# Local attention beside a gated MLP: sixteen half-position units with interleaved logits, and the first fold over the taps on GpSimd

## The chip, the cores and the metric

The kernel runs on one core of a Trainium2 chip. The metric is the device time of one execution in microseconds. The engines are TensorE (PE in the profile, its weight loads PEld), VectorE (DVE), ScalarE (ACT), GpSimd (POOL) and SyncE (SP), whose queue issues most of the transfers. Each engine works through its own instructions in the order in which they stand in the program, and waits at an instruction until the semaphores that it needs have come.

## The reference

```python
def _A_ref(x, wqkv, wo):                       # S 2048, D 512, 32 heads of 16
    q, k, v = ...                              # x @ wqkv, split by head
    idx = pos[:, None] - (jnp.arange(8) * 2)[None, :]      # eight taps, two positions apart
    logits = jnp.einsum("bhsd,bhswd->bhsw", q, k[idx]) * scale   # masked where idx < 0
    o = jnp.einsum("bhsw,bhswd->bhsd", _softmax(logits), v[idx])
    return o.reshape(B, S, D) @ wo

def _B_ref(x, w_in, w_sp, b_sp, w_out):        # F 1792, half of it 896
    z = _gelu(x @ w_in)
    z1, z2 = z[..., :Fh], _layernorm(z[..., Fh:])
    g = jnp.einsum("ts,bsf->btf", w_sp, z2) + b_sp[None, :, None]
    return (z1 * g) @ w_out

xn = _layernorm(x)
out = x + _A_ref(xn, wqkv, wo) * silu(_B_ref(xn, w_in, w_sp, b_sp, w_out))
```

Every position attends to itself and to seven positions before it, each two further back. There is no long product in this attention: its sums are short, and they are made with elementwise operations, one head of 16 channels at a time.

## The kernel before

All matrix products are made from a high and a low part of each float32 operand, three matmuls in place of one (high by high, high by low, low by high). ScalarE rounds the high part (`split`, L183) and VectorE subtracts to get the low part (L184). Weights pass through four raw buffers and eight pairs of split buffers (`weight_pair`, `fetch`, `prep`). The stages are, in the order of TensorE's work: the QKV products (L371 to L373), written to memory in `qkv_d`; z1 (L578 to L580); z2 with its layer norm (L606 to L627), whose statistics end with four small operations on GpSimd (L620 to L623); the spatial product in blocks (`three`, L695), partly by sums of blocks; the projection by `w_out` (`proj`, named b, L910 to L912); and the projection of attention by `wo` (also `proj`, named s), by groups of four position slots in the order 0, 2, 3, 1, each loaded with `load_o` (L678) from `o_d`.

Positions lie as `(p j)`: partition p holds positions 16 p to 16 p + 15, and j from 0 to 15 is the slot. The attention works on eight sets of 64 channels (four heads each), one after the other, in `attention(sub)`. It loads q, and windows of k and v with 14 positions of halo. For each of four groups of four slots it multiplies all eight taps of k by q (L503, tile `pr`, 128x2048) and sums each head's 16 channels (L506). Then it makes the softmax over the taps for all sixteen slots at once (L513 to L525, the exponential on ScalarE at L521). Then, for each group of four slots, it multiplies the taps of v by the weights (L530, in the same buffer `pr`), folds eight taps to four (L536), to two (L537) and to one (L538), transposes in blocks of 32 (L545), and stores with four transfers to `o_d` (L548).

The order of instructions on each engine is worked out when the kernel is built, from priorities. The attention has the lowest one (`LOW`), so it fills VectorE where nothing for TensorE is due. All of the attention's tiles have one buffer, `tt` has two.

Of the kernel before, what the change touches and what calls it, by code (L numbers as in the profile page):

```python
# [11 lines left out]
F32 = mybir.dt.float32  # L12
F32R = mybir.dt.float32r
AF = mybir.ActivationFunctionType
ALU = mybir.AluOpType
AX = mybir.AxisListType

P = 128
# [3 lines left out]
H, DH, W, DIL = 32, 16, 8, 2  # L22
NT = S // P
# [10 lines left out]
NSUB = 8  # L34
CS = D // NSUB
Q = 32
HS = CS // DH
NBLK = GC // CS
HALO = (W - 1) * DIL
NJ = 4  # L40
PAD = 16
WIN = NT + HALO
EPS = 1e-5
MASKED = -1e9 * float(DH) ** 0.5
LOW = 1_000_000
# [4 lines left out]
SYNC = mybir.DependencyInfo(mybir.DependencyClass.Sync, mybir.DependencyReason.DATA)  # L50
# [4 lines left out]
def kernel(  # L55
# [13 lines left out]
    nc = tc.nc  # L69
# [20 lines left out]
    qkv_d = dram.tile([3 * NSUB, S + PAD, CS], F32, name="qkv_d")  # L90
# [6 lines left out]
    o_d = dram.tile([NSUB, NT // NJ, CS, P // Q, NJ * Q], F32, name="o_d")  # L97
# [11 lines left out]
    mask = const.tile([P, W, NT], F32, name="mask")  # L109
# [363 lines left out]
        return t.rearrange("p (i t) -> p i t", i=2)[:, :n]  # L473

    ap_ = ctx.enter_context(tc.tile_pool(name="att", bufs=1))
    at_priority = [LOW]

    def attention(sub):
        saved = tc.cur_priority
        tc.cur_priority = at_priority[0]  # L480
        q = ap_.tile([P, NT, CS], F32, tag="q", name=f"q_{sub}")
        kw = ap_.tile([P, WIN, CS], F32, tag="k", name=f"k_{sub}")
        vw = ap_.tile([P, WIN, CS], F32, tag="v", name=f"v_{sub}")

        def window(t):
            b = qkv_d[3 * sub + t, PAD - HALO :, :]
            return bass.AP(tensor=b.tensor, offset=b.offset, ap=[[NT * CS, P], [1, WIN * CS]])

        nc.sync.dma_start(kw.rearrange("p r c -> p (r c)"), window(1))
        nc.sync.dma_start(q, qkv_d[3 * sub, PAD:, :].rearrange("(p j) c -> p j c", j=NT))  # L490
        nc.sync.dma_start(vw.rearrange("p r c -> p (r c)"), window(2))

        def taps(t, j0):
            b = t[:, j0 : j0 + 1, :]
            return bass.AP(
                tensor=b.tensor, offset=b.offset, ap=[list(b.ap[0]), [DIL * CS, W], [1, NJ * CS]]
            )

        lg = ap_.tile([P, W, NT * HS], F32, tag="lg", name=f"lg_{sub}")
        for j0 in range(0, NT, NJ):  # L500
            pr = ap_.tile([P, W, NJ * CS], F32, tag="pr", name=f"pr_{sub}_{j0}")
            qb = q[:, j0 : j0 + NJ, :].rearrange("p j c -> p (j c)")
            nc.vector.tensor_tensor(  # L503
                pr, taps(kw, j0), qb.unsqueeze(1).to_broadcast([P, W, NJ * CS]), op=ALU.mult
            )
            nc.vector.tensor_reduce(  # L506
                lg[:, :, j0 * HS : (j0 + NJ) * HS],
                pr.rearrange("p w (i d) -> p w i d", d=DH),
                axis=AX.X,
                op=ALU.add,  # L510
            )
        lgv = lg.rearrange("p w (j h) -> p w j h", h=HS)
        nc.vector.tensor_tensor(  # L513
            lgv, lgv, mask.unsqueeze(3).to_broadcast([P, W, NT, HS]), op=ALU.add
        )
        mx = ap_.tile([P, NT * HS], F32, tag="mx", name=f"mx_{sub}")
        nc.vector.tensor_reduce(mx, lg.rearrange("p w i -> p i w"), axis=AX.X, op=ALU.max)
        nc.vector.tensor_tensor(
            lg, lg, mx.unsqueeze(1).to_broadcast([P, W, NT * HS]), op=ALU.subtract
        )  # L520
        nc.scalar.activation(lg, lg, AF.Exp, scale=float(DH) ** -0.5)  # L521
        sm = ap_.tile([P, NT * HS], F32, tag="sm", name=f"sm_{sub}")
        nc.vector.tensor_reduce(sm, lg.rearrange("p w i -> p i w"), axis=AX.X, op=ALU.add)
        nc.vector.reciprocal(sm, sm)
        nc.vector.tensor_tensor(  # L525
            lg, lg, sm.unsqueeze(1).to_broadcast([P, W, NT * HS]), op=ALU.mult
        )
        for j0 in range(0, NT, NJ):
            pr = ap_.tile([P, W, NJ * CS], F32, tag="pr", name=f"pv_{sub}_{j0}")
            nc.vector.tensor_tensor(  # L530
                pr.rearrange("p w (i d) -> p w i d", d=DH),
                taps(vw, j0).rearrange("p w (i d) -> p w i d", d=DH),
                lg[:, :, j0 * HS : (j0 + NJ) * HS].unsqueeze(3).to_broadcast([P, W, NJ * HS, DH]),
                op=ALU.mult,
            )
            nc.vector.tensor_tensor(pr[:, 0:4], pr[:, 0:4], pr[:, 4:8], op=ALU.add)  # L536
            nc.vector.tensor_tensor(pr[:, 0:2], pr[:, 0:2], pr[:, 2:4], op=ALU.add)  # L537
            nc.vector.tensor_tensor(  # L538
                pr[:, 2].rearrange("p (b j c) -> p j b c", b=CS // Q, j=NJ),
                pr[:, 0].rearrange("p (j b c) -> p j b c", b=CS // Q, j=NJ),  # L540
                pr[:, 1].rearrange("p (j b c) -> p j b c", b=CS // Q, j=NJ),
                op=ALU.add,
            )
            tt = ap_.tile([P, CS // Q, NJ * Q], F32, tag="tt", name=f"tt_{sub}_{j0}", bufs=2)
            nc.vector.transpose(tt.rearrange("p b x -> p (b x)"), pr[:, 2])  # L545
            for a in range(P // Q):
                dst = o_d[sub, j0 // NJ, :, a]
                nc.sync.dma_start(  # L548
                    dst.rearrange("(b c) x -> c b x", c=Q), tt[a * Q : (a + 1) * Q]
                )  # L550
        at_priority[0] = tc.cur_priority
        tc.cur_priority = saved

    for sub in range(NSUB):
        attention(sub)

    def block_sums(i):
        top, low = t4(f"sa_{i}"), t4(f"sb_{i}")
# [52 lines left out]
    def spatial_block(c, js):  # L611
        return prep(w_sp[c, js], CT, f"wsp_{c}_{js}")
# [104 lines left out]
    for c in (2, 3):  # L717
        for n, js in enumerate(order):
            w = spatial.get((c, js)) or spatial_block(c, js)
# [11 lines left out]
        for f0 in range(0, FB, 2):  # L731
            n = min(2, FB - f0)
# [183 lines left out]
    for i, j in enumerate(rows_of):  # L916
        c, jj = divmod(j, JC)
# [29 lines left out]
    for i in range(0, NT, 2):  # L947
        j0 = rows_of[i]
# [67 lines left out]
```

## Time and profile before

| | before |
|---|---|
| median of two timed runs | 708.0 us (707.93 and 708.08) |
| span of the profiled execution | 706.6 us |
| TensorE busy | 700.7 us, 3152 matmuls |
| VectorE busy | 619.2 us |
| ScalarE busy | 260.9 us |
| GpSimd busy | 41.8 us |
| moved by transfers | 151.93 MB |

The span reaches from the first to the last instruction of one profiled execution; no separate time of that execution is given, so it stands beside the median of the timed runs, 1.4 us below it. A group's row in the profile gives line, engine, operation, tiles and shapes, the count, then the busy time in us and the mean in ns, then the engine's idle time just before these instructions and what ended it. A row of the timeline gives the start in us, the duration in us, engine, line and operation. A row of waits gives who waited for whom, the total in us, how often, and the longest. Engine and share rows are told where they stand.

### The profile page before, as it was taken

What the parts mean: (1) busy time and instruction counts of PE and PEld (TensorE: products, weight loads), DVE (VectorE), ACT (ScalarE), POOL (GpSimd) and SP (SyncE); (2) the same over time, 40 slices, a digit from 0 to 9 for tenths busy, and PEclk for the clock granted to TensorE, in tenths of its full rate; (3) what the DMA queues carried; (4) which work ended last, traced back from release to release, by engine and by line L of the source; (5) the groups of instructions that cost most, each with busy time, mean ns of one, the idle gap of its engine ahead of it and who ended that gap; (6) DMA issues with size and microseconds to landing.
All of it is one profiled execution on the core that took longest, in us unless ns stands there. A gap on an engine that the chain in (4) does not pass through costs nothing.

```text
span 706.6 us, 8920 instructions
## 1 busy us (share of the span) xinstructions
PE 700.7 (99%) x3152; PEld 585.4 (83%) x3152; DVE 619.2 (88%) x770; ACT 260.9 (37%) x403; POOL 41.8 (6%) x81
## 2 busy tenths in 40 slices
PE   8999999999999999999999999999999999999997
PEld 7888888888888988888888888888888888888886
DVE  6774599989998899989999999999999999799665
ACT  4343332343224466751112211354545542131531
POOL 3100000000000443320000000000000000000000
PEclk9999999999999999999999999999999999999999
DMA  8767775585785131579956742877857781353996
GB/s 271 255 189 228 240 242 178 161 287 207 258 275 220 33 135 69 190 255 323 328 183 219 288 135 60 307 239 260 276 200 269 246 260 59 125 165 101 303 327 235
DMA packets 96652, 151.93 MB, mean 215 GB/s; under 512 B 8672, under 2 KB 50912, under 8 KB 96608
## 3 DMA queue, kind: packets, MB, share of 16 engines
q1 hardware_dynamic: 57968, 108.77, 47.1%
q10 hardware_dynamic: 38640, 42.60, 17.3%
q8 instruction: 24, 0.39, 0.2%
q14 instruction: 20, 0.16, 0.1%
HBM read 100.40 MB, written 50.94 MB: 214 GB/s over the span
## 4 chain that ended last, share of the span: by engine, by line
PE 98%; DMA 1%; DVE 0%; SPq 0%; issue 0%
PE g L695 22%; PE q L695 12%; PE p L695 6%; PE qkv L371 6%; PE qkv L373 6%; PE qkv L372 6%; PE z L608 4%; PE z L607 4%; PE z L606 4%; PE z L580 4%; PE b L911 4%; PE z L578 4%; PE b L910 4%; PE b L912 4%; PE z L579 4%; PE s L911 2%
## 5 line engine op out<-in xcount | busy, mean ns | idle before, releaser
L503 DVE TENSOR_TENSOR pr<-k,q 128x2048 f32<-128x2048 f32 x32 | 73.2, 2286 | 1.9 <-DMA q<-qkv_d 1.5
L530 DVE TENSOR_TENSOR pv<-v,lg 128x2048 f32<-128x2048 f32 x32 | 73.3, 2291 | 0.9
L506 DVE TENSOR_REDUCE lg<-pr 128x128 f32<-128x2048 f32 x32 | 73.0, 2281 | 0.4
L391 ACT ACTIVATE stage<-qkv 128x512 f32<-128x512 f32 x36 | 21.4, 596 | 49.2 <-PE qkv L373 49.1
L536 DVE TENSOR_TENSOR pv<-pv 128x1024 f32<-128x1024 f32 x32 | 39.1, 1221 | 0.5
L608 PE MATMUL z<-w_0h,BIG 128*128 128x512 f32 x64 | 25.0, 391 | 0.0
L607 PE MATMUL z<-w_0l,BIG 128*128 128x512 f32 x64 | 25.0, 391 | 0.0
L606 PE MATMUL z<-w_0h,BIG 128*128 128x512 f32 x64 | 24.9, 389 | 0.0
L921 ACT ACTIVATE bt<-b 128x512 f32<-128x512 f32 x16 | 9.4, 597 | 41.5 <-PE b L912 41.5
L627 ACT ACTIVATE zt<-zt,nmz,mvz 128x896 f32<-128x896 f32 x16 | 17.9, 1134 | 17.6 <-POOL nmz L623 17.3
L267 DVE TENSOR_TENSOR xT<-xT,mr 128x512 f32<-128x512 f32 x20 | 13.8, 688 | 11.2 <-DMA mr<-mv_d 6.6
L537 DVE TENSOR_TENSOR pv<-pv 128x512 f32<-128x512 f32 x32 | 22.0, 687 | 0.6
L608 PE MATMUL z<-w_1h,BIG 128*128 128x384 f32 x64 | 21.5, 336 | 0.0
L606 PE MATMUL z<-w_1h,BIG 128*128 128x384 f32 x64 | 21.5, 335 | 0.0
L607 PE MATMUL z<-w_1l,BIG 128*128 128x384 f32 x64 | 21.4, 335 | 0.0
L587 ACT ACTIVATE z1t<-z 128x512 f32<-128x512 f32 x21 | 12.5, 594 | 21.8 <-PE z L580 21.8
L965 DVE TENSOR_TENSOR sg<-s,sg 128x512 f32<-128x512 f32 (+1 forms) x17 | 11.2, 657 | 10.6 <-PE s L912 9.7
L618 DVE BATCH_NORM_STATS2 zst<-zt 128x6 f32<-128x448 f32 x32 | 19.1, 610 | 1.5 <-ACT zt L609 1.5
L620 POOL TENSOR_TENSOR nmz<-mvz,mone 128x1 f32<-128x1 f32 x16 | 5.0, 315 | 234.8 <-DVE mvz L619 234.7
L184 DVE TENSOR_TENSOR BIG<-zt,BIG 128x896 fp32r<-128x896 f32 x16 | 17.1, 1079 | 1.1 <-ACT BIG L183 1.1
L609 ACT ACTIVATE zt<-z 128x512 f32<-128x512 f32 (+1 forms) x24 | 12.8, 535 | 13.4 <-PE z L608 12.1
L373 PE MATMUL qkv<-wqkv_0h,BIG 128*128 128x512 f32 x43 | 16.7, 389 | 0.0
(543 smaller groups left out, 2164.1 us busy)
## 6 DMA issues: line engine op xcount, KB each, us to landing
qkv_d<-stage ACTq DMA_DIRECT2D x24, 512.0 KB
k<-qkv_d SPq DMA_DIRECT2D x8, 960.0 KB
v<-qkv_d SPq DMA_DIRECT2D x8, 960.0 KB
z_d<-z1t ACTq DMA_DIRECT2D x14, 512.0 KB
t_d<-zt ACTq DMA_DIRECT2D x16, 384.0 KB
zl<-z_d SPq DMA_DIRECT2D x12, 512.0 KB
tr<-t_d SPq DMA_DIRECT2D x16, 384.0 KB
x<-in_x SPq DMA_DIRECT2D x16, 256.0 KB
```

What stands on the lines that cost most here:

```text
L371: nc.tensor.matmul(pq, xh[:, k], wh, start=k == 0, stop=False)
L372: nc.tensor.matmul(pq, xh[:, k], wl, start=False, stop=False)
L373: nc.tensor.matmul(pq, xl[:, k], wh, start=False, stop=k == KB - 1)
L503: nc.vector.tensor_tensor(pr, taps(kw, j0), qb.unsqueeze(1).to_broadcast([P, W, NJ * CS]), op=ALU.mult)
L506: nc.vector.tensor_reduce(lg[:, :, j0 * HS : (j0 + NJ) * HS], pr.rearrange("p w (i d) -> p w i d", d=DH), axis=AX.X, op=ALU.add,)
L530: nc.vector.tensor_tensor(pr.rearrange("p w (i d) -> p w i d", d=DH), taps(vw, j0).rearrange("p w (i d) -> p w i d", d=DH), lg[:, :, j0 * ...
L536: nc.vector.tensor_tensor(pr[:, 0:4], pr[:, 0:4], pr[:, 4:8], op=ALU.add)
L606: nc.tensor.matmul(pz, xh[:, k], wh, start=k == 0, stop=False)
L607: nc.tensor.matmul(pz, xh[:, k], wl, start=False, stop=False)
L608: nc.tensor.matmul(pz, xl[:, k], wh, start=False, stop=k == KB - 1)
L695: nc.tensor.matmul(pg, z[a], w[b], start=start and i == 0, stop=stop and i == 2, skip_group_check=seeded)
L911: nc.tensor.matmul(pp[:, cols], hi, wl, start=False, stop=False)
```

## The change

The eight sets of channels become sixteen units: each set is cut into its slots 0 to 7 and 8 to 15. A unit loads half of q and windows of k and v with 22 instead of 30 positions per partition, and makes its softmax over eight slots. The units overlap: while unit u makes its weighted sums, the logits of unit u + 1 are made between them, one group of four slots at a time. For that, `pv` (weighted products) gets a buffer of its own beside `pr` (products of logits), `lg` gets two buffers, and `tt` goes from two buffers to one. The first fold, eight taps to four, moves from VectorE to GpSimd, and a dependency is added by hand so that it starts after the following unit's product of logits, beside the sum over channels. The rest of a weighted sum (`finish`) follows after that sum over channels.

```diff
+        def first_fold(part, after=None):
+            pv = part[2]
+            ins = nc.gpsimd.tensor_tensor(pv[:, 0:4], pv[:, 0:4], pv[:, 4:8], op=ALU.add)
+            if after is not None:
+                tc.add_manual_dep(ins.ins, after.ins.name, SYNC, reason="beside the sum over channels")
...
-            nc.vector.tensor_tensor(pr[:, 0:4], pr[:, 0:4], pr[:, 4:8], op=ALU.add)
...
-            tt = ap_.tile([P, CS // Q, NJ * Q], F32, tag="tt", name=f"tt_{sub}_{j0}", bufs=2)
+            tt = ap_.tile([P, CS // Q, NJ * Q], F32, tag="tt", name=f"tt_{u}_{j0}", bufs=TTB)   # TTB = 1
...
+        def start(u):
+            load_qk(u)
+            lgs[u] = ap_.tile([P, W, NH * HS], F32, tag="lg", name=f"lg_{u}", bufs=2)
+
+        start(0)
+        for j0 in range(0, NH, NJ):
+            heads(0, j0, scores(0, j0)[0])
+        load_v(0)
+        softmax(0)
+        part = None
+        for u in range(len(units)):
+            more = u + 1 < len(units)
+            if more:
+                start(u + 1)
+            for j0 in range(0, NH, NJ):
+                if more:
+                    pr, ins = scores(u + 1, j0)
+                    if part:
+                        first_fold(part, ins)
+                    heads(u + 1, j0, pr)
+                elif part:
+                    first_fold(part)
+                if part:
+                    finish(part)
+                part = weighted(u, j0)
+            if more:
+                load_v(u + 1)
+                softmax(u + 1)
+        first_fold(part)
+        finish(part)
```

`scores` is the product of L503 and `heads` the sum of L506, `weighted` the product of L530, and `finish` holds L537 to L548; in `softmax` the operations of L513 to L525 stand as they were, on half the slots.

More of the change, by code (lines that the diff above doesn't have):

```diff
@@ L41 @@
 PAD = 16
-WIN = NT + HALO
+NH = NT // 2
+HWIN = NH + HALO
+TTB = 1
 EPS = 1e-5
@@ L475, with attention, window, load_qk @@
     ap_ = ctx.enter_context(tc.tile_pool(name="att", bufs=1))
-    at_priority = [LOW]
-    def attention(sub):
+    def attention():
         saved = tc.cur_priority
[L480 to L491, printed above, removed]
+        tc.cur_priority = LOW
+        units = [(sub, h) for sub in range(NSUB) for h in range(2)]
+        qs, ks, vs, lgs = {}, {}, {}, {}
+        def window(sub, t, h):
+            b = qkv_d[3 * sub + t, PAD - HALO + h * NH :, :]
+            return bass.AP(tensor=b.tensor, offset=b.offset, ap=[[NT * CS, P], [1, HWIN * CS]])
+        def load_qk(u):
+            sub, h = units[u]
+            ks[u] = ap_.tile([P, HWIN, CS], F32, tag="k", name=f"k_{sub}_{h}")
+            qs[u] = ap_.tile([P, NH, CS], F32, tag="q", name=f"q_{sub}_{h}")
+            nc.sync.dma_start(ks[u].rearrange("p r c -> p (r c)"), window(sub, 1, h))
+            nc.sync.dma_start(
+                qs[u],
+                qkv_d[3 * sub, PAD:, :].rearrange("(p j) c -> p j c", j=NT)[:, h * NH : (h + 1) * NH],
+            )
+        def load_v(u):
+            sub, h = units[u]
+            vs[u] = ap_.tile([P, HWIN, CS], F32, tag="v", name=f"v_{sub}_{h}")
+            nc.sync.dma_start(vs[u].rearrange("p r c -> p (r c)"), window(sub, 2, h))
         def taps(t, j0):
@@ L497, in taps, with scores, heads @@
             )
[L499 to L504, printed above, removed]
-            )
+        def scores(u, j0):
+            pr = ap_.tile([P, W, NJ * CS], F32, tag="pr", name=f"pr_{u}_{j0}")
+            qb = qs[u][:, j0 : j0 + NJ, :].rearrange("p j c -> p (j c)")
+            ins = nc.vector.tensor_tensor(
+                pr, taps(ks[u], j0), qb.unsqueeze(1).to_broadcast([P, W, NJ * CS]), op=ALU.mult
+            )
+            return pr, ins
+        def heads(u, j0, pr):
             nc.vector.tensor_reduce(
-                lg[:, :, j0 * HS : (j0 + NJ) * HS],
+                lgs[u][:, :, j0 * HS : (j0 + NJ) * HS],
                 pr.rearrange("p w (i d) -> p w i d", d=DH),
@@ L511, in attention @@
             )
[L512 to L533, printed above, removed]
+        def softmax(u):
+            sub, h = units[u]
+            n = NH * HS
+            lg = lgs[u]
+            lgv = lg.rearrange("p w (j h) -> p w j h", h=HS)
+            mk = mask[:, :, h * NH : (h + 1) * NH]
+            nc.vector.tensor_tensor(
+                lgv, lgv, mk.unsqueeze(3).to_broadcast([P, W, NH, HS]), op=ALU.add
+            )
+            mx = ap_.tile([P, n], F32, tag="mx", name=f"mx_{u}")
+            nc.vector.tensor_reduce(mx, lg.rearrange("p w i -> p i w"), axis=AX.X, op=ALU.max)
+            nc.vector.tensor_tensor(
+                lg, lg, mx.unsqueeze(1).to_broadcast([P, W, n]), op=ALU.subtract
+            )
+            nc.scalar.activation(lg, lg, AF.Exp, scale=float(DH) ** -0.5)
+            sm = ap_.tile([P, n], F32, tag="sm", name=f"sm_{u}")
+            nc.vector.tensor_reduce(sm, lg.rearrange("p w i -> p i w"), axis=AX.X, op=ALU.add)
+            nc.vector.reciprocal(sm, sm)
+            nc.vector.tensor_tensor(
+                lg, lg, sm.unsqueeze(1).to_broadcast([P, W, n]), op=ALU.mult
+            )
@@ L534, in attention, with weighted @@
+        def weighted(u, j0):
+            pv = ap_.tile([P, W, NJ * CS], F32, tag="pv", name=f"pv_{u}_{j0}")
+            nc.vector.tensor_tensor(
+                pv.rearrange("p w (i d) -> p w i d", d=DH),
+                taps(vs[u], j0).rearrange("p w (i d) -> p w i d", d=DH),
+                lgs[u][:, :, j0 * HS : (j0 + NJ) * HS].unsqueeze(3).to_broadcast([P, W, NJ * HS, DH]),
                 op=ALU.mult,
             )
-            nc.vector.tensor_tensor(pr[:, 0:4], pr[:, 0:4], pr[:, 4:8], op=ALU.add)
+            return u, j0, pv
@@ L537, in attention, with finish @@
+        def first_fold(part, after=None):
[3 more added lines that the diff above has]
+                tc.add_manual_dep(ins.ins, after.ins.name, SYNC, reason="beside the sum over channels")
+        def finish(part):
+            u, j0, pr = part
+            sub, h = units[u]
             nc.vector.tensor_tensor(pr[:, 0:2], pr[:, 0:2], pr[:, 2:4], op=ALU.add)
@@ L543, in attention @@
             )
-            tt = ap_.tile([P, CS // Q, NJ * Q], F32, tag="tt", name=f"tt_{sub}_{j0}", bufs=2)
+            tt = ap_.tile([P, CS // Q, NJ * Q], F32, tag="tt", name=f"tt_{u}_{j0}", bufs=TTB)
             nc.vector.transpose(tt.rearrange("p b x -> p (b x)"), pr[:, 2])
             for a in range(P // Q):
-                dst = o_d[sub, j0 // NJ, :, a]
+                dst = o_d[sub, (h * NH + j0) // NJ, :, a]
                 nc.sync.dma_start(
@@ L550, in attention @@
                 )
-        at_priority[0] = tc.cur_priority
+        def start(u):
[27 more added lines that the diff above has]
+        finish(part)
         tc.cur_priority = saved
-    for sub in range(NSUB):
-        attention(sub)
+    attention()
     def block_sums(i):
```

## The prediction

> **What bounds the kernel now.** I read the engine shares first, then the chain that ended last, the list of TensorE's waits and the busy time by stage.
>
> ```profile
> PE 700.7 (99%) x3152; PEld 585.4 (83%) x3152; DVE 619.2 (88%) x770; ACT 260.9 (37%) x403; POOL 41.8 (6%) x81
> PE 98%; DMA 1%; DVE 0%; SPq 0%; issue 0%
> PE warm L276 <- POOL ident masks.py:199: 1.3, 1, 1.3
> 216.00:306.00 90.00, 90.00 (x441) 80.01 (x440) 85.75 (x122) 52.08 (x73) 28.33 (x58) 1.00 0.33 117
> 583.00:659.00 76.00, 76.00 (x337) 62.94 (x336) 68.56 (x71) 21.36 (x35) 0.00 (x0) 1.00 0.37 123
> 659.00:707.00 48.00, 43.99 (x206) 36.73 (x204) 26.62 (x36) 13.13 (x17) 0.00 (x0) 0.99 0.87 289
> ```
>
> TensorE is busy for 700.7 of 706.6 us, carries 98% of the chain, and its longest wait is the 1.3 us at the very start. In the stage rows (length, then PE, PEld, DVE, ACT and POOL busy, clock, DMA share) it is busy for all 90.00 and 76.00 us. The 5.9 us that it is not busy lie in the opening and after the last product. The granted clock is 1.00, so there is nothing to win there either. VectorE is nearly as full, but ahead of TensorE: the attention is what fills it.
>
> So the change, which touches no product, can win about 1 us at the most. What is to be worked out is whether it makes TensorE wait. The span is 706.6 us and the median of the two timed runs 708.0; the 1.4 us between them I carry over unchanged. A measurement of this kernel can tell about 2% from no change, which is 14.2 us.
>
> **Where attention meets TensorE.** The last unit must be stored, loaded back and split before the output projection reaches its rows. From the timeline, VectorE, SyncE's queue and TensorE:
>
> ```profile
> 658.20 0.45 DVE L545 STREAM_TRANSPOSE tt<-pv 128x256 f32<-128x256 f32 x1
> 662.02 1.90 SPq L548 DMA_DIRECT2D o_d<-tt  x4
> 676.95 0.69 DVE L184 TENSOR_TENSOR o_3l<-ol,o_3h 128x512 fp32r<-128x512 f32 x1 [3.23 <-ACT o_3h L183]
> 682.95 0.39 PE L910 MATMUL s<-BIG,o_3h 128*128 128x512 f32 x1
> ...
> 663.22 0.69 DVE L184 TENSOR_TENSOR o_3l<-ol,o_3h 128x512 fp32r<-128x512 f32 x1 [0.45 <-ACT o_3h L183]
> 672.07 0.39 PE L910 MATMUL s<-BIG,o_3h 128*128 128x512 f32 x1
> ```
>
> The last transpose ends at 658.65. Its store stands in SyncE's queue until 662.02 (3.4 us), the split ends at 677.64, and the product starts at 682.95 (5.3 us): 8.7 us in hand. The group of rows before it has 672.07 - 663.91 = 8.2 us. Attention may end about 8 us later than now before TensorE waits; every further microsecond is one of the whole time.
>
> **The change part by part**, as X, the shift of attention's end. First VectorE's groups and GpSimd's two nearest:
>
> ```profile
> L530 DVE TENSOR_TENSOR pv<-v,lg 128x2048 f32<-128x2048 f32 x32 | 73.3, 2291 | 0.9
> L503 DVE TENSOR_TENSOR pr<-k,q 128x2048 f32<-128x2048 f32 x32 | 73.2, 2286 | 1.9 <-DMA q<-qkv_d 1.5
> L506 DVE TENSOR_REDUCE lg<-pr 128x128 f32<-128x2048 f32 x32 | 73.0, 2281 | 0.4
> L536 DVE TENSOR_TENSOR pv<-pv 128x1024 f32<-128x1024 f32 x32 | 39.1, 1221 | 0.5
> L537 DVE TENSOR_TENSOR pv<-pv 128x512 f32<-128x512 f32 x32 | 22.0, 687 | 0.6
> L538 DVE TENSOR_TENSOR pv<-pv 128x256 f32<-128x256 f32 x32 | 13.5, 420 | 0.7
> L545 DVE STREAM_TRANSPOSE tt<-pv 128x256 f32<-128x256 f32 x32 | 14.2, 443 | 0.7
> L288 POOL TENSOR_TENSOR wqkv_3l<-wqkv_3r,wqkv_3h 128x512 fp32r<-128x512 f32 x1 | 1.3, 1300 | 0.0
> L620 POOL TENSOR_TENSOR nmz<-mvz,mone 128x1 f32<-128x1 f32 x16 | 5.0, 315 | 234.8 <-DVE mvz L619 234.7
> ```
>
> Removed from VectorE: the first fold, L536, 32 x 1.221 = -39.1 us. The products, sums over channels, other folds and transposes keep their number and shapes.
>
> Added on GpSimd: 32 folds of 128x1024. No such operation stands in the trace. Twice the 1.300 of 128x512 is 2.60; with the fixed part counted once (0.315, from 128x1) it is 2.60 - 0.315 = 2.29. I take 2.29, the sum over channels beside it takes 2.281: nearly the same. 29 folds stand beside such a sum, three do not (the last of unit 14, both of unit 15).
>
> The softmax is made 16 times at half size. A 128x256 operation takes 0.420 (L538), and its rows of now are
>
> ```profile
> L523 DVE TENSOR_REDUCE sm<-lg 128x64 f32<-128x512 f32 x8 | 8.6, 1078 | 6.4 <-ACT lg L521 6.4
> L518 DVE TENSOR_TENSOR lg<-lg,mx 128x512 f32<-128x512 f32 x8 | 5.5, 684 | 0.1
> L627 ACT ACTIVATE zt<-zt,nmz,mvz 128x896 f32<-128x896 f32 x16 | 17.9, 1134 | 17.6 <-POOL nmz L623 17.3
> ```
>
> so 2 x 0.420 - 0.684 = 0.156 for each pair of halves; six operations, eight times: +7.5 us (3.7 if only the three two-input ones pay it, about 12 at twice that for the others). The wait for the exponential, 6.4 us over eight, becomes sixteen shorter ones: between 0 and +6.4, I take +3.2.
>
> **The port.** GpSimd and VectorE get into each other's way, and the trace shows when. Four pictures, the second column is the duration:
>
> ```profile
> 285.07 0.22 POOL L621 TENSOR_SCALAR mvz<-mvz 128x1 f32<-128x1 f32 x1
> 284.83 2.28 DVE L506 TENSOR_REDUCE lg<-pr 128x128 f32<-128x2048 f32 x1
> ...
> 296.19 0.67 POOL L621 TENSOR_SCALAR mvz<-mvz 128x1 f32<-128x1 f32 x1
> 296.09 0.68 DVE L184 TENSOR_TENSOR wsp_9l<-wsp_9r,wsp_9h 128x512 fp32r<-128x512 f32 x1
> 296.69 0.68 DVE L184 TENSOR_TENSOR wsp_2l<-wsp_2r,wsp_2h 128x512 fp32r<-128x512 f32 x1
> ...
> 10.43 1.30 POOL L288 TENSOR_TENSOR wqkv_3l<-wqkv_3r,wqkv_3h 128x512 fp32r<-128x512 f32 x1
> 11.06 0.96 DVE L208 TENSOR_SCALAR x<-x,mvx 128x512 f32<-128x512 f32 x1
> L208 DVE TENSOR_SCALAR x<-x,mvx x4: 477/482/960, 4.9 to 14.0; 128x512 f32<-128x512 f32 x4
> ```
>
> Beside a sum over channels GpSimd's small operation takes 0.22. Beside a two-input VectorE operation the same one takes 0.67 and ends at 296.86, just behind the end of that operation at 296.77, although VectorE's next had already begun. The other way round, L208 takes 0.96 instead of 0.48 while a GpSimd operation runs until 11.73. So a fold beside the sum over channels should cost nothing but the handover: the bounds are 0 and 0.5 (a fold of 2.60 and the signals), I take 0.2 for 16 folds, +3.2.
>
> The other 13 meet something else. Splits for TensorE come between a product and its sum wherever they are due:
>
> ```profile
> 95.89 2.29 DVE L503 TENSOR_TENSOR pr<-k,q 128x2048 f32<-128x2048 f32 x1
> 98.10 0.69 DVE L184 TENSOR_TENSOR w_0l<-w_0r,w_0h 128x512 fp32r<-128x512 f32 x1
> 98.70 0.68 DVE L184 TENSOR_TENSOR w_1l<-w_1r,w_1h 128x512 fp32r<-128x512 f32 x1
> ...
> 99.90 2.28 DVE L506 TENSOR_REDUCE lg<-pr 128x128 f32<-128x2048 f32 x1
> ```
>
> Counted over the timeline, two or more two-input operations follow 14 of the 32 products directly, so 13 of 29 folds. There the fold slips in behind the first split and the second waits for all of it. The bounds are 0 (VectorE keeps the port) and 13 x 2.3 = 29.9; I take the upper, since at 296.86 GpSimd came in between two such operations.
>
> [...]
>
> The last unit has no logits beside it. Its two folds stand bare between product and second fold: 2 x 2.5 = +5.0.
>
> X = -39.1 + 7.5 + 3.2 + 3.2 + 29.9 + 5.0 = +9.7. Less the 8.2 in hand, TensorE waits 1.5 us: 708.0 + 1.5 = **709.5 us**.
>
> **What I cost at nothing.** The loads: k is single-buffered and free only after the unit's last product of logits; a sum, the folds, a weighted product and a softmax follow (2.3 + 1.6 + 2.3 + 4.2 = 10.4 us) before its successor is needed.
>
> ```profile
> L489 SPq DMA_DIRECT2D k<-qkv_d x8: 320/327/338, 75.5 to 531.1; - x8
> 81.95 2.29 DVE L503 TENSOR_TENSOR pr<-k,q 128x2048 f32<-128x2048 f32 x1 [1.51 <-DMA q<-qkv_d]
> ACT wsp_14h L183 <- PE g L695: 6.7, 2, 4.1
> SPq L548 <- DVE tt L545: 89.1, 24, 10.2
> ```
>
> The first load, of bigger tiles, took 75.5 to 81.95, 6.4 us. Without that cover (SyncE's queue late) each of 15 units loses up to the load's own 6.4 us. The single tt: transposes come 8.6 us apart (one turn of 2.29 + 2.28 + 0.69 + 0.42 + 0.44 + 2.29), four stores take 1.9 us to issue. VectorE waiting for a fold holds back the splits queued behind it, and TensorE waits for those; but ScalarE's half of a split waits up to 4.1 us for TensorE to release a weight, so the eight pairs are filled as far ahead as they go. GpSimd's statistics of z2 now queue behind folds, and L627 already waits 17.3 us for them without TensorE noticing; 2.3 more now and then lie under the eight banks of its output.
>
> **The rivals.** (1) The port costs little, X is between -39.1 + 3.7 + 5.0 = -30 (all lower bounds) and +8: TensorE feels nothing, **708.0**. For it: 12 of the 32 products are followed by their sum at once. Against it: the 29.9. (2) The order on VectorE and SyncE's queue is fixed when the kernel is built. If it was laid out without the port, VectorE lags it by 29.9 + 3.2 = 33 us late in the kernel, and the splits lag with it, as do the weights' loads behind the stores (10.2 us of head-of-line wait already). Seven pairs of weights with nine products each (76.00 us over 337 products, 0.226 us each) lead by 7 x 9 x 0.226 = 14 us: TensorE would wait 33 - 14 = 19, **727**. It decides from a lag of 14 us. Against it: idle time of VectorE (7.4 us in 583 to 659) takes lag back. (3) On the other side most strongly: the folds do not run beside anything, because the sum over channels is also held or GpSimd starts late. Then VectorE stands 32 x 2.5 = 80 us; X = -39.1 + 7.5 + 3.2 + 80 = +51.6, and 51.6 - 8.2 = 43 us of waiting, **751**; it passes 2% from X = 22. Against it: the 0.22 beside a sum. [...]
>
> **How the numbers follow.** Forecast, 708.7 to 714: 0.44. Rival 1: 0.33. Rival 2: 0.13, two thirds of it over 722. Rival 3: 0.10. Slower by over 2%: 0.09 + 0.10 = 0.19; faster by over 2%, which would need fewer products: 0.01; within: 0.80. The range reaches from 706.8 (a microsecond of the opening's waits gone) to 727 (rival 2), which leaves rival 3 and the upper edge of 2 outside.
>
> **What would show it.** Folds of about 2.3 us on GpSimd, 29 of them under L506's successor; VectorE's second fold waiting some 0.2 us on GpSimd; splits of 2.5 to 3 us instead of 0.69 directly behind products of logits, about 13; the last transpose near 668; TensorE without a gap until 670 and with 1 to 2 us at the o tiles. I am wrong if TensorE waits for weights before 580 (rival 2), if the sums grow beyond 2.3 us (rival 3), or if the last transpose is over 15 us from 668.

## The result and the profile after

The changed kernel takes **740.17 us** (two runs, 739.41 and 740.94) beside 708.0: the ratio is 1.0454, 95% interval 1.0424 to 1.0484. It is slower by 32 us, outside the predicted range. The profiled execution took 740.94 us, its span is 739.2 us.

The page of after: engine shares, the chain by engine, and the groups of the fold, of the sums over channels and of the second fold.

```profile
PE 714.3 (97%) x3152; PEld 593.4 (80%) x3152; DVE 613.9 (83%) x786; ACT 264.9 (36%) x417; POOL 135.1 (18%) x113
...
PE 40%; DVE 33%; DMA 14%; issue 9%; ACT 1%; SPq 1%; POOL 1%; DVEq 0%; ACTq 0%; POOLq 0%
...
L560 POOL TENSOR_TENSOR pv<-pv 128x1024 f32<-128x1024 f32 x32 | 93.2, 2913 | 422.0 <-DVE pv L550 356.6
...
L519 DVE TENSOR_REDUCE lg<-pr 128x128 f32<-128x2048 f32 x32 | 72.6, 2270 | 0.1
...
L567 DVE TENSOR_TENSOR pv<-pv 128x512 f32<-128x512 f32 x32 | 21.7, 678 | 0.9 <-POOL pv L560 0.7
```

TensorE carried 98% of the chain, now 40%. It does the same 3152 products, yet is busy 714.3 - 700.7 = 13.6 us longer; and it is not busy for 739.2 - 714.3 = 24.9 us, where it was 5.9. The two, 13.6 + 19.0, are the whole 32.6 us between the spans. TensorE's waits in after:

```profile
PE z L666 <- DVE w_1l L186: 4.2, 1, 4.2
PE g L754 <- ACT g L773: 3.5, 1, 3.5
PE q L754 <- ACT va L941: 3.3, 1, 3.3
PE g L754 <- ACT zt L668: 3.2, 1, 3.2
PE p L754 <- ACT p L773: 3.1, 1, 3.1
```

Five waits of 3.1 to 4.2 us; two of 0.6 follow further down. By the timeline the seven begin at 225, 303, 386, 470, 493, 570 and 625: the long ones where one stage hands over to the next. (L665 to L667 are the products of z2, L754 the spatial product, L773 the ScalarE operation that seeds a bank of it, L668 the activation that empties a bank of z2.) The busy time around the five long ones, from after's stretches (length, then PE, PEld, DVE, ACT and POOL busy, clock, DMA share, GB/s):

```profile
218.00:236.00 18.00, 13.53 (x55) 11.76 (x54) 17.91 (x20) 5.98 (x10) 5.77 (x2) 0.81 0.96 329
...
300.00:312.00 12.00, 8.81 (x35) 7.14 (x34) 12.00 (x16) 9.16 (x15) 4.57 (x5) 0.86 0.23 78
312.00:384.00 72.00, 72.00 (x320) 59.63 (x319) 67.60 (x94) 21.67 (x31) 20.73 (x20) 1.00 0.84 286
384.00:396.00 12.00, 8.46 (x27) 6.43 (x26) 12.00 (x17) 4.05 (x7) 0.00 (x0) 0.72 0.85 290
...
468.00:480.00 12.00, 8.88 (x33) 6.82 (x32) 11.90 (x15) 2.36 (x4) 0.95 (x1) 0.86 0.88 332
...
566.00:580.00 14.00, 10.72 (x34) 8.03 (x33) 14.00 (x19) 7.02 (x12) 4.14 (x1) 0.76 0.73 240
```

Between the waits the clock is 1.00, as before; in the five stretches that hold a long wait it is 0.72 to 0.86. From the starts of the products, against 0.227 us from one to the next elsewhere (0.174 for the products of 384 columns, which follow the first wait), those behind the five waits lost 2.40, 1.64, 2.67, 1.71 and 2.88 us, 11.3 in all. That is most of the 13.6. I did not take the rest apart; by an estimate a little over 1 us of it is the last product before each of the seven waits, whose row of 0.39 us (the one at 469.66, for example) counts whole, where elsewhere the next product starts after 0.227. VectorE is busy in all of these stretches.

Two places in after's timeline show what made VectorE late (start, duration, engine, line):

```profile
208.40 0.68 DVE L626 TENSOR_TENSOR sb<-sa,sb 128x512 f32<-128x512 f32 x1
209.00 2.61 DVE L537 TENSOR_TENSOR lg<-lg,mx 128x256 f32<-128x256 f32 x1
...
208.62 2.71 POOL L560 TENSOR_TENSOR pv<-pv 128x1024 f32<-128x1024 f32 x1 [15.09 <-DVE pv L550]
...
378.73 2.88 DVE L186 TENSOR_TENSOR wsp_2l<-wsp_2r,wsp_2h 128x512 fp32r<-128x512 f32 x1
...
378.61 2.45 POOL L560 TENSOR_TENSOR pv<-pv 128x1024 f32<-128x1024 f32 x1 [14.12 <-DVE pv L550]
```

L537, a two-input operation of 128x256 like the L538 of 0.420 us in the prediction, takes 2.61, a split of 0.68 takes 2.88: each ends just behind the fold (211.61 behind 211.33, 381.61 behind 381.06), 2.2 us late. Twenty VectorE operations are held by a fold like this, each over 0.3 us too long, for 39.1 us over their usual durations; 8.3 us of it have gathered before 225, 11.8 before 303, 17.4 before 386, 25.4 before 470, 31.5 before 570. (The expectations below say 19 and 37 us; the twentieth is a split of `wout` at 605.86.) And GpSimd's longest waits show why the folds do not stand where they were meant to:

```profile
POOL pv L560 <- DVE pv L550: 356.6, 30, 28.9
```

The added dependency lets a fold start after the product of logits L513. But 30 folds are released by their own weighted product L550: in the built order it stands behind the product of logits, so the dependency is met long before. Only 11 of the 32 folds have a sum over channels beside them.

### The profile page after: what moved, and what is told of

Its sections match the earlier page's. It is cut to its first block, busy times and chain, and to the rows that moved or that the text cites. A ratio compares the mean times of both kernels' runs of the same rounds, so it can differ in the third digit from the quotient of the medians.

```text
span 739.2 us, 9084 instructions
## 1 busy us (share of the span) xinstructions
PE 714.3 (97%) x3152; PEld 593.4 (80%) x3152; DVE 613.9 (83%) x786; ACT 264.9 (36%) x417; POOL 135.1 (18%) x113
## 4 chain that ended last, share of the span: by engine, by line
PE 40%; DVE 33%; DMA 14%; issue 9%; ACT 1%; SPq 1%; POOL 1%; DVEq 0%; ACTq 0%; POOLq 0%
PE q L754 7%; DVE pv L550 5%; DVE pr L513 5%; DVE lg L519 3%; PE b L970 3%; PE b L971 3%; PE b L969 3%; PE p L754 3%; PE z L666 2%; DVE BIG L186 2%; PE z L667 2%; PE z L665 2%; PE qkv L373 2%; PE qkv L375 2%; PE qkv L374 2%
## 5 line engine op out<-in xcount | busy, mean ns | idle before, releaser
L560 POOL TENSOR_TENSOR pv<-pv 128x1024 f32<-128x1024 f32 x32 | 93.2, 2913 | 422.0 <-DVE pv L550 356.6
L513 DVE TENSOR_TENSOR pr<-k,q 128x2048 f32<-128x2048 f32 x32 | 77.0, 2406 | 3.8 <-DMA q<-qkv_d 1.8
L550 DVE TENSOR_TENSOR pv<-v,lg 128x2048 f32<-128x2048 f32 x32 | 72.7, 2273 | 0.1
L665 PE MATMUL z<-w_0h,BIG 128*128 128x512 f32 x64 | 25.1, 392 | 0.0
L667 PE MATMUL z<-w_0h,BIG 128*128 128x512 f32 x64 | 25.0, 391 | 0.0
L186 DVE TENSOR_TENSOR o_1l<-ol,o_1h 128x512 fp32r<-128x512 f32 x3 | 2.1, 688 | 26.8 <-ACT o_1h L185 26.8
L665 PE MATMUL z<-w_1h,BIG 128*128 128x384 f32 x64 | 22.3, 349 | 0.2 <-ACT w_1h L185 0.2
L667 PE MATMUL z<-w_1h,BIG 128*128 128x384 f32 x64 | 22.4, 350 | 0.0
L626 DVE TENSOR_TENSOR sb<-sa,sb 128x512 f32<-128x512 f32 x16 | 15.3, 959 | 6.1 <-DMA sb<-in_w_sp 6.1
L754 PE MATMUL g<-wsp_0h,BIG 128*128 128x512 f32 x28 | 12.0, 459 | 6.7 <-ACT g L773 3.5
L540 ACT ACTIVATE lg<-lg 128x256 f32<-128x256 f32 x16 | 6.6, 414 | 31.2 <-DVE lg L537 31.1
```

Source lines behind the costliest of these rows:

```text
L186: pin(nc.vector.tensor_tensor(lo, src, hi.bitcast(F32), op=ALU.subtract))
L513: ins = nc.vector.tensor_tensor(pr, taps(ks[u], j0), qb.unsqueeze(1).to_broadcast([P, W, NJ * CS]), op=ALU.mult)
L550: nc.vector.tensor_tensor(pv.rearrange("p w (i d) -> p w i d", d=DH), taps(vs[u], j0).rearrange("p w (i d) -> p w i d", d=DH), lgs[u][:, : ...
L560: ins = nc.gpsimd.tensor_tensor(pv[:, 0:4], pv[:, 0:4], pv[:, 4:8], op=ALU.add)
L665: nc.tensor.matmul(pz, xh[:, k], wh, start=k == 0, stop=False)
L667: nc.tensor.matmul(pz, xl[:, k], wh, start=False, stop=k == KB - 1)
```

## The experiments

My theory: a GpSimd fold holds VectorE's two-input operations, VectorE comes late to the handovers, TensorE waits there and then runs slow. The rivals: the new order and the sixteen units do it without any holding; or the wait for the slower fold does. The prediction and the expectations speak of "the port" for this holding; the runs show which operations are held and for how long, not what the two engines share.

**The same order, without the fold's reads.** f1_write_only gives VectorE, ScalarE, GpSimd and SyncE the order of after, instruction by instruction, and puts a write in place of the fold. The first fold is thus left out of its result.

```diff
-            ins = nc.gpsimd.tensor_tensor(pv[:, 0:4], pv[:, 0:4], pv[:, 4:8], op=ALU.add)
+            ins = nc.gpsimd.memset(pv[:, 0:8], 0.01)
...
+        for a, b in zip(order, order[1:]):          # order: after's, for each of the four engines
+            tc.add_manual_dep(traced[b], traced[a].name, NS, reason="the order of another plan")
```

> The changed kernel with the order of every engine but TensorE fixed to the one it was built with, and one instruction replaced: GpSimd's first fold becomes a write of a constant into the same tile (no read; the first fold is left out of the result). Theory port: VectorE is late because two-input operations stand still for whole folds (19 of them, 37 us in all, each 1.1 to 2.2 us too long). A GpSimd instruction that only writes holds nobody up, so no two-input operation is over 0.3 us too long, TensorE's waits of over 3 us are gone, 707 to 710 us. Rival order: the fixed order of the sixteen units starves TensorE at the stage boundaries by itself; the order is unchanged, so 730 to 741 us with the same five long waits.

Measured: 709.46 us, ratio 1.0022 (1.0009 to 1.0036). The page and the only wait of TensorE behind the opening:

```profile
PE 701.2 (99%) x3152; PEld 585.9 (83%) x3152; DVE 574.4 (81%) x786; ACT 266.7 (38%) x417; POOL 100.2 (14%) x113
...
L560 POOL MEMSET pv<- 128x2048 f32 x32 | 58.0, 1814 | 418.6 <-DVE pv L550 352.3
```

```profile
PE g L754 <- ACT g L773: 0.3, 1, 0.3
```

The memset starts behind the same L550 and occupies GpSimd for 1.81 us, 32 times, in 21 of them for over 1 us beside two-input operations, but no operation of VectorE is held by it (L537 takes 0.42 us in the mean, a split of `wsp` 0.67 to 0.70). 30.7 of the 32 us are gone with the order unchanged, so the order alone is not the cause. The memset is also shorter than the fold, so in itself this run could mean that the wait for the fold costs; but in after VectorE's second fold waited for GpSimd only 0.7 us in all 32 times. What is left is that the fold reads and adds, where the memset only writes: a split beside the fold took 2.88 us in after where it usually takes 0.68, and none is held beside the 32 memsets here.

**The sixteen units with the fold on VectorE.** e1_fold_on_vector, planned anew:

```diff
-            ins = nc.gpsimd.tensor_tensor(pv[:, 0:4], pv[:, 0:4], pv[:, 4:8], op=ALU.add)
-            if after is not None:
+            ins = nc.vector.tensor_tensor(pv[:, 0:4], pv[:, 0:4], pv[:, 4:8], op=ALU.add)
+            if False:
```

> The sixteen units as they are, the first fold back on VectorE without the added dependency; the order is planned anew. Theory port: no operation is held, VectorE has 39 us more of its own work than in the changed kernel and 37 less of standing still, TensorE waits under 3 us in all, 708 to 712 us, and attention ends between 650 and 670. Rival order (units and interleaving): long waits at the stage boundaries stay, 720 to 740 us.

Measured: 708.45 us, ratio 1.0000 (0.9991 to 1.0009). Its last transpose in the timeline:

```profile
641.11 0.45 DVE L575 STREAM_TRANSPOSE tt<-pv 128x256 f32<-128x256 f32 x1
```

Units, interleaving and half softmaxes cost nothing. With all the work still on VectorE attention ends 17 us earlier than before (658.20), earlier than I expected too, and the time does not move: nothing waited for that end.

**The fold in four pieces.** e3_small_folds:

```diff
-            ins = nc.gpsimd.tensor_tensor(pv[:, 0:4], pv[:, 0:4], pv[:, 4:8], op=ALU.add)
+            for i in range(4):
+                ins = nc.gpsimd.tensor_tensor(pv[:, i], pv[:, i], pv[:, 4 + i], op=ALU.add)
...
```

> The fold as four GpSimd instructions of 128x256, planned anew. Theory port: whoever waits, waits for one of them only, so each held operation is at most 0.8 us too long instead of 2.2, but more of them are held; in all 10 to 30 us, 712 to 732 us. Rival order: 735 to 745 us.

Measured: 728.42 us, ratio 1.0283 (1.0262 to 1.0303). Its timeline at one fold, and TensorE's two longest waits:

```profile
131.92 2.84 DVE L513 TENSOR_TENSOR pr<-k,q 128x2048 f32<-128x2048 f32 x1
...
131.82 4.95 POOL L561 TENSOR_TENSOR pv<-pv 128x256 f32<-128x256 f32 x4 [9.16 <-DVE pv L550]
```

```profile
PE z L670 <- DVE w_1l L186: 4.8, 1, 4.8
PE g L758 <- ACT wsp_8h L185: 2.4, 1, 2.4
```

One piece runs and holds L513 by 0.56 us (2.84 for 2.28); the other three come only behind that product, which ends at 134.76, and are done at 136.77. So the hold here is about as long as one piece: the three take 2.01 us, 0.67 each, against holds of 2.2 us beside the whole folds above. There are more holds now, 49, together 25.9 us: less than 39.1, and the time lies between.

**Sums put behind the products by hand.** f2_beside fixes VectorE's order as the attention is written, each sum straight behind its product of logits. The fold stays on GpSimd.

```diff
+ORDER = {'DVE': [...]}      # attention in written order, each sum over channels behind its product
...
+            tc.add_manual_dep(traced[b], traced[a].name, NS, reason="the order of another plan")
```

> The changed kernel with VectorE's order fixed by hand: the attention's instructions in the order in which they are written, in the places that they had, and each sum over channels moved directly behind its product of logits, so that 29 of 32 folds find it beside them (now about 13 do). The fold stays on GpSimd and reads. Theory port: held two-input operations fall from 19 to at most 5, 8 us in all, TensorE's long waits are gone or down to one, 708 to 715 us. Rival order: another order of the same units starves it as well, 725 to 745 us. If the fold and the sum over channels exclude each other after all, the sums grow to 4 us and more and the time passes 745.

Measured: 739.21 us, ratio 1.0439 (1.0423 to 1.0454). The held time fell as expected, to three operations and 4.5 us in all, and the time did not: a miss. **f5_beside_write** is the same order with the memset of f1 in place of the fold:

> The kernel whose VectorE order was fixed by hand (folds beside the sums, 739 us), with GpSimd's fold turned into a write of a constant of the same tile; the first fold is left out. If that order itself starves TensorE, as no operation was held there: 722 to 740 us. If GpSimd's reading did it in some way that the durations don't show: 707 to 714 us.

Measured: 732.52 us, ratio 1.0340 (1.0318 to 1.0362). TensorE's longest waits, first f2_beside, then f5_beside_write, and the timeline of f2_beside in between:

```profile
PE g L754 <- ACT zt L668: 11.8, 2, 7.8
```

```profile
303.52 2.23 DVE L550 TENSOR_TENSOR pv<-v,lg 128x2048 f32<-128x2048 f32 x1
306.15 2.28 DVE L513 TENSOR_TENSOR pr<-k,q 128x2048 f32<-128x2048 f32 x1
...
303.68 2.12 POOL L679 TENSOR_TENSOR nmz<-mvz,mone 128x1 f32<-128x1 f32 x1 [0.88 <-DVE mvz L678]
306.39 2.46 POOL L681 TENSOR_TENSOR mvz<-mvz,nhalf 128x1 f32<-128x1 f32 x1
```

```profile
PE g L754 <- ACT zt L668: 11.7, 2, 7.9
```

The two kernels wait alike, so it is this order by hand, and not the fold, that costs there: 24 of the 31 us of f2 are already in f5. It pays no heed to when things are due. It puts a weighted product and a product of logits among z2's statistics; GpSimd's small operations take 2.12 and 2.46 us beside them, ScalarE's normalisation waits for these (2.41 us at 309.16), and its emptying of a bank comes in line after that (at 314.70, behind a store of `zt` that it waited 3.42 us for). f2 therefore doesn't say what a fold beside a sum costs.

**The same placement, known to the planner.** f4_beside_planned takes after, keeps each product of logits behind the weighted product written ahead of it, and puts whatever stood between a product and its sum behind that sum; the rest is planned anew with these edges in place.

```diff
+            if behind is not None:
+                tc.add_manual_dep(ins.ins, behind.ins.name, NOSYNC, reason="kept behind the weighted product")
...
+    for later, earlier in EDGES:                    # 155 pairs
+        tc.add_manual_dep(traced[later], traced[earlier].name, NS, reason="behind the sum over channels")
```

> The changed kernel planned anew with two kinds of order edges and no new wait: each product of logits behind the weighted product written before it, and 155 edges that put whatever VectorE was planned to do between a product of logits and its sum behind that sum. So 29 folds stand beside a sum over channels, and the plan knows the order, unlike in the run where it was fixed by hand (739 us). Theory port: no operation is held over 0.7 us, TensorE's long waits are gone, 708 to 714 us. Rival (an order that keeps folds beside sums costs TensorE as much as the holds do, since splits wait for whole sums): 720 to 740 us.

Measured: 712.45 us, ratio 1.0049 (1.0031 to 1.0068). Its timeline at a fold beside a sum, then at one of the three folds that have no sum beside them; and TensorE's waits:

```profile
368.37 2.28 DVE L514 TENSOR_TENSOR pr<-k,q 128x2048 f32<-128x2048 f32 x1
370.69 2.29 DVE L522 TENSOR_REDUCE lg<-pr 128x128 f32<-128x2048 f32 x1
...
370.80 2.41 POOL L563 TENSOR_TENSOR pv<-pv 128x1024 f32<-128x1024 f32 x1 [11.20 <-DVE pr L514]
...
544.85 2.62 DVE L187 TENSOR_TENSOR q_7l<-q_7r,q_7h 128x512 fp32r<-128x512 f32 x1
...
544.53 2.38 POOL L563 TENSOR_TENSOR pv<-pv 128x1024 f32<-128x1024 f32 x1 [17.61 <-DVE pv L553]
```

```profile
PE q L757 <- DVE q_7l L187: 1.3, 1, 1.3
PE q L757 <- DVE q_6l L187: 2.1, 1, 2.1
```

All 29 folds that have a sum to stand beside do so; the sum takes its 2.29 us and the fold 2.41, and 17 operations behind such a sum take 0.16 to 0.19 us too long (at 501.60 a split of 0.95 takes 1.13). This is the price that the prediction put on them: nearly nothing. The three bare ones still hold splits, for 1.9 to 2.2 us each where I expected none over 0.7, and one of these, q_7l, is waited for at once. 27.7 of the 32 us are back, with the fold on GpSimd.

**The bare folds on VectorE.** f6_last_on_vector adds to f4:

```diff
-            ins = nc.gpsimd.tensor_tensor(pv[:, 0:4], pv[:, 0:4], pv[:, 4:8], op=ALU.add)
+            eng = nc.gpsimd if after is not None else nc.vector
+            ins = eng.tensor_tensor(pv[:, 0:4], pv[:, 0:4], pv[:, 4:8], op=ALU.add)
```

> The version planned anew with folds beside sums (712.5 us), and the three folds that have no sum beside them back on VectorE. Theory port: the two operations of the last unit that were held for 2 us are free, TensorE's wait of 1.3 us near 546 is gone, the one of 2.1 us near 505 (a chain of splits behind a sum) may stay, 709 to 712 us. Rival (that wait comes from the order too): 712 to 714 us.

Measured: 712.67 us, ratio 1.0066 (1.0047 to 1.0086), no better than f4, as the rival has it. The wait for q_7l is gone, as is the hold. The one at 505 us stays: q_6l in f6_last_on_vector, and the busy time there, first f4_beside_planned, then f6_last_on_vector:

```profile
PE q L758 <- DVE q_6l L187: 2.4, 1, 2.4
```

```profile
500.00:512.00 12.00, 9.87 (x44) 7.85 (x43) 12.00 (x18) 3.45 (x6) 1.92 (x1) 1.00 0.84 274
```

```profile
500.00:512.00 12.00, 9.58 (x36) 7.51 (x35) 12.00 (x17) 3.50 (x6) 2.32 (x1) 0.86 0.79 254
```

A wait of 2.13 us left the clock at 1.00; one of 2.42 brought it to 0.86 and cost another 1.55 us. What makes q_6l late at 505 is the new plan itself, with no fold holding it; I did not take that further.

**Waits put into the kernel before.** c1_pause_short and c2_pause_long put pauses into z2 of the kernel before: a small product that needs 2 or 12 copies of ScalarE. Nothing else changes but the edges that keep the pause in its place.

```diff
+        for n in range(12):                         # 2 in c1_pause_short
+            nc.scalar.activation(slack, src[:, HALF[1]][:, :P], AF.Copy)
+        m = nc.tensor.matmul(pp[:, :P], slack, ident, start=True, stop=True)
```

> The same six pauses with two small copies in place of twelve, some 1.2 to 1.6 us each. Theory: so short a wait leaves the clock alone, 6 x 1.4 = 8 us, 714 to 718 us. Rival: the clock drops after any wait, 722 us and more.

> The kernel before, with six pauses of TensorE put into the z2 stage: a small product that needs a chain of twelve small ScalarE copies behind the last activation of the step, some 3.5 to 4 us each. It measures what a wait costs beyond its own length. Theory: after a wait of over 3 us the granted clock drops and the next 8 to 15 products take up to 0.3 us too long, 1.6 to 2.9 us more each time, so 6 x 3.8 + 6 x 2.3 = 37 us, 738 to 750 us. Rival: a wait costs its length only, 727 to 733 us.

Measured: 716.44 us (1.0113, 1.0091 to 1.0135) and 735.09 us (1.0376, 1.0354 to 1.0399). The pauses came out uneven, and c2 stays below what was expected. TensorE's wait for its pauses in c2_pause_long, and its stretches around the two longest:

```profile
PE pause L621 <- ACT slack L620: 14.8, 4, 7.4
```

```profile
258.00:274.00 16.00, 11.24 (x42) 9.35 (x41) 13.13 (x17) 9.05 (x19) 4.70 (x8) 0.79 0.17 58
284.00:300.00 16.00, 8.63 (x35) 6.99 (x34) 14.20 (x17) 10.15 (x20) 5.69 (x8) 0.79 0.39 143
```

Waits alone, with no fold on GpSimd, bring the lower clock with them, here 0.79. The products lost 2.8 us behind the wait of 4.76, 1.4 behind that of 7.37, 1.7 behind one of 1.95 and 0.15 behind one of 2.02; in c1, 1.7 behind one of 2.52. So c1 came out in its range, but not by its theory: a wait under 3 us did not leave the clock alone (0.88 from 260 to 274 in c1). Each of the five waits of after cost half to nine tenths as much again in clock, and in c2 what a wait cost was not proportional to its length.

**Only the fold, in the old order.** e4_subs_gpsimd is the kernel before with L536 on GpSimd, planned anew.

```diff
-            nc.vector.tensor_tensor(pr[:, 0:4], pr[:, 0:4], pr[:, 4:8], op=ALU.add)
+            nc.gpsimd.tensor_tensor(pr[:, 0:4], pr[:, 0:4], pr[:, 4:8], op=ALU.add)
```

> The kernel before with one edit: the first fold on GpSimd, in the eight sets as they were, planned anew. Nothing is made to run beside it. Theory port: most of the 32 folds hold a two-input operation, 25 to 60 us of standing in all, TensorE waits at the same boundaries, 722 to 750 us. Rival (only the sixteen units with it do harm): under 714 us.

Measured: 722.78 us, ratio 1.0204 (1.0183 to 1.0224). TensorE's longest wait, and VectorE's for the fold:

```profile
PE g L695 <- ACT g L714: 4.2, 1, 4.2
```

```profile
DVE pv L537 <- POOL pv L536: 44.2, 19, 2.6
```

Here VectorE often stands idle beside the fold (44.2 us), and an idle engine can't be held: 9 operations are, 16.1 us, where I expected most of the 32 folds to hold one. Moving the fold alone costs 14.5 us. That the fuller VectorE of after made it dearer is my reading; no run shows it by itself.

## Why the prediction was wrong

**"TensorE waits at the o tiles": the wrong place.** The forecast followed X, the shift of attention's end, against 8.2 us in hand. The last transpose in after:

```profile
629.84 0.43 DVE L575 STREAM_TRANSPOSE tt<-pv 128x256 f32<-128x256 f32 x1
```

It ends at 630.27, 28 us earlier than before, where I had it at 668. X was a sum of busy times, as if VectorE's work stood in one row behind the last transpose. But the attention has the lowest priority and the planner spreads it: already e1, with no less work on VectorE, ends 17 us earlier. The end decided next to nothing in any run: TensorE's only wait at the o tiles is one of 0.8 us, in e4_subs_gpsimd.

**"Seven pairs lead by 14 us": the step that failed.** Lateness of VectorE stood under "What I cost at nothing", because the weights are filled far ahead. At a handover TensorE does not wait for the next pair. It waits for a short chain: VectorE empties a bank, ScalarE seeds it, the product starts. The kernel before, its timeline:

```profile
369.19 0.68 DVE L739 TENSOR_TENSOR gt<-g,bb 128x512 f32<-128x512 f32 x1
...
369.91 0.60 ACT L714 ACTIVATE g<-bb 128x512 f32<-128x512 f32 x1 [2.95 <-DVE gt L739]
...
373.56 0.39 PE L695 MATMUL g<-wsp_0h,BIG 128*128 128x512 f32 x1
```

The seed ends at 370.51 and the product that needs it comes at 373.56: a lead of 3.05 us, not 14, and it could be read in the profile of before. The same place in after:

```profile
388.07 0.68 DVE L798 TENSOR_TENSOR gt<-g,bb 128x512 f32<-128x512 f32 x1
...
388.78 0.60 ACT L773 ACTIVATE g<-bb 128x512 f32<-128x512 f32 x1 [5.46 <-DVE gt L798]
...
389.44 0.79 PE L754 MATMUL g<-wsp_0h,BIG 128*128 128x512 f32 x1 [3.54 <-ACT g L773]
```

Now the seed is the last to come, 3.54 us too late. At 225 it is a split itself that is late, since there the pair needed is the last of its stage. The first long wait came with 8.3 us of held time, below the 14 from which rival 2 was to decide.

**"13 held splits, 2.3 us each, 29.9 us": size near, reason not.** It was 20 operations and 39.1 us, 1.96 each. But I counted places where two two-input operations follow a product of logits, in the order of before, and expected the folds there. (Of the 14 products counted 11 have them straight behind; three have them further on before the sum. And of the rows that the exclusion rested on, that of 0.96 us is of an operation with one input.) The new order put folds behind weighted products instead, and so 21 of 32 had no sum beside them. A dependency says what a fold may not precede, not what it will stand beside. Why the planner chose this I can only argue: `pv` has one buffer, its rest waits for the fold, and it filled the time with the next product.

**"The handover, 3.2 us; the second fold waits 0.2": right where a fold stands beside a sum.** The fold took 2.41 where I had 2.29, the sum beside it 2.29 (f4). Rival 3, sums held as well, falls: in after they take 2.27 us in the mean.

**"The softmax halves": right.** A two-input operation took 0.41 (I had 0.42), and the reduction L542

```profile
212.61 0.61 DVE L542 TENSOR_REDUCE sm<-lg 128x32 f32<-128x256 f32 x1
```

twice is 0.14 over the 1.078 of the whole one (I had 0.156). Together the six operations took 6.7 us more (I had 7.5). The wait for the exponential did not grow by 3.2 us, though: it fell from 6.4 to 2.8, outside my bounds. And the turn between two transposes adds up to 8.4 us, not 8.6; nothing hung on that.

**Rival 2, 727 us, held the mechanism** (VectorE lags a fixed order and TensorE waits on the way) but had 0.13. It priced the waits at 33 less 14, 19 us; TensorE's time without work did grow by 19.0. That is not a confirmation, since the waits come from five separate handovers and not from one lag less one lead. What it lacked altogether is TensorE's 13.6 us more of busy time: no step of mine asked what a wait does to the clock. With it the sum would have been 741.

**How the question stands.** Shown: the fold costs 30.7 us more at the order of after than a write in its place (f1); without the move nothing is lost (e1); beside the sums most comes back (f4). Not shown one by one: which held operation made which handover late. And no version beat 708.0: TensorE has no microsecond to give.

## What to carry to other kernels

A two-input operation moved to GpSimd was nearly free here only beside an operation that it did not hold: 2.29 us for the sum over channels and 2.41 for the fold beside it in f4, while each operation held in after lost 1.96 us in the mean. So look in the built order at what releases it and at what runs while it does. The slack of a nearly full engine that feeds another is read at the handovers between stages, at the last link of the chain that the first product there needs (3.05 us here, where I had 14), and not from how far the weights are filled ahead. And the waits of 3.1 to 4.2 us on TensorE are to be priced with half to nine tenths as much again, for the products behind them ran slower (clock 0.72 to 0.86 in those stretches).

## What the runs showed of the hardware

- **Between two VectorE operations GpSimd can come in.** At 209.00 in after L537 had been next in line on VectorE directly behind L626, and the fold, begun 0.38 us earlier, ended first, at 211.33 before 211.61. It took 2.71 us there, beside L626 until 209.08; beside a sum over channels it takes 2.41 (f4). But it does not always come in: the fold begun at 584.21 in e4_subs_gpsimd took 7.54 us, since the eight splits behind the running one went first, at 0.68 us each. The operations do not decide it: between the same two splits (one of `zl`, then `wout_0l`) the fold came in at 605.49 in after and did not at 608.03 in f2_beside; and in after alone, between a split of q and one of `tr`, it came in at 537.20 (2.72 us) and did not at 568.84 (4.14 us). What does decide it stays open, and the upper bound that the prediction took from one such place was a choice that the traces bear out only in part.
- **It goes both ways.** GpSimd's operations on one number per partition took 0.18 to 0.60 us from 299.89 to 302.62 in f2_beside, but 2.12 beside VectorE's weighted product and 2.46 beside its product of logits.
- **The clock fell behind waits below three microseconds, and not behind all of them.** Behind 2.42 (f6), 2.52 (c1) and 1.95 us (c2, clock 0.72 from 252 to 258) of waiting it cost 1.55, 1.7 and 1.7 us; behind 2.13 (f4) 0.11, and behind another 2.52 (f2_beside, clock 1.00 from 286 to 299) 0.2. In c2 another wait of 2.02 us left it at 1.00 (300 to 316). What sets the edge these runs do not settle.
